# Pooled attention in other tiles (queries 64, 64, 16; keys 128 and 16), and a planner with corrected durations

## The chip, the cores and the metric

The kernel runs on one core of a Trainium2 chip. The metric is the time of one execution on the device in microseconds (us). The engines are TensorE (PE: matmuls, and PEld for its weight loads), VectorE (DVE), ScalarE (ACT), GpSimd (POOL) and the DMA queues, which are issued here by SyncE (SP) and POOL. All inputs and the output are in HBM. PE reads SBUF and writes PSUM; DVE and ACT read and write both.

## The reference

An attention layer over 8 batches, 8 heads, 576 positions and 64 elements a head, and a gated feed-forward network (the code calls it moe) over its 4,608 rows. The weights come as float64.

```python
def _attn_ref(q, k, v):
    factor = 4
    q_d = q.reshape(B, H, Sd, factor, D).mean(axis=3)      # Sd = 144 pooled positions; k_d, v_d likewise
    out_d = sm_attn(q_d, k_d, v_d)                         # softmax attention over the pooled positions
    out_up = np.repeat(out_d, factor, axis=2)
    mask = np.abs(pos[:, None] - pos[None, :]) < factor    # a band of 7 keys
    out_local = softmax(where(mask, scale * q @ k.T, -1e9)) @ v
    return out_up + out_local

def _moe_ref(x, w1, w2, w3, w_out):
    return ((x @ w1) * (x @ w2) @ w3) @ w_out
```

So each row of the network's input is the sum of pooled attention (144 by 144 for each of the 64 batch-heads) and local attention in a band.

## The kernel before, in words

*Network.* `fold` multiplies w3 by w_out once (`accw`, 128 instructions on PE), which leaves one matrix `wphl`. The rows are worked through in 12 chunks of 384 (`moe(c)`). In each, for 8 blocks of the hidden width, PE forms the two gate products (`pab`, L269 to L271, three matmuls per block of the contraction as every operand is split in a high and a low part), ACT copies one (L912), DVE multiplies it with the other (L914), ACT and DVE split the product (L919, L921), and PE multiplies it with `wphl` into `acc`. ACT copies the results (L929) and SP stores them. The split inputs `xh`, `xl` of a chunk are written by two "units" of 192 rows (L861, L862).

*Local attention.* For batches 0 and 1 (`PB`) it is done on PE in groups (`group_unit`, `group_scores`, `group_values`: `se_ps`, `te_ps`, `oe_ps`). These need the queries with the four members of a pool side by side; `turn` in `pooled_sums` makes that order (L559, on ACT). For batches 2 to 7 it is done by `unit` on DVE and ACT: 7 products (L767), reductions (L777, L780), a small softmax, 7 products with v (L826, L834) and their sum, three of the additions being DMAs that POOL issues and that accumulate into `xl` (L842).

*Pooled attention*, the part that is changed. `pooled(b)` brings the sums of q and k over the four members of each pool into `qks` and the sums of v into `vs`: SP issues a first load, POOL three accumulating DMAs (L433, L434; for batches 0 and 1 DVE sums q and k). v lies in `vs` as 72 partitions by 2 halves of the keys. Then `quad` runs twice a batch, for 4 heads each: the scores in three tiles of queries that start at 0, 48 and 80 and are 64 long, two pairs of heads one below the other in 128 partitions, so the tiles overlap (`s_ps`, L482); maxima on DVE (L487), exponentials on ACT with their sums (L496: 6 a quad), the division by the sums on ACT (L508, batches 0 and 1) or POOL (L511); 12 transposes on PE (`t_ps`, L521), because the two halves of 72 keys are transposed apart; and copies into `pt` on ACT (L528). The last step, `values`, multiplies `pt` by v in 32 products over 72 keys (`o_ps`, L449), and ACT copies the result to `oup` (L457, L459).

*Order.* Nothing runs in the order in which it is written. Each piece is a task with an engine, a cost in us, the tasks it needs and the buffers it takes. `Plan.order` simulates the engines with these costs, forward and backward in several rounds, picks the order that its replays find shortest, and the tasks are then issued in that order. Each engine works through its own list in order and waits for semaphores.

Of the kernel before, what the change touches and what calls it, by code (L numbers as in the profile page):

```python
# [32 lines left out]
NT = 3  # L33
THIRDS = [(0, 0), (48, 0), (80, 16)]
# [28 lines left out]
AHEAD = 4  # L63

# [15 lines left out]
class Task:  # L80
    __slots__ = ("eng", "cost", "fn", "deps", "late", "rings", "after")

    def __init__(self, eng, cost, fn, deps, late, rings, after):
        self.eng, self.cost, self.fn, self.deps, self.late, self.rings, self.after = eng, cost, fn, deps, late, rings, after


class Plan:

    def __init__(self):
        self.tasks = []  # L90

    def add(self, eng, cost, fn, deps=(), take=(), uses=(), late=0.0):
# [7 lines left out]
        t = Task(eng, cost, fn, [d for d in deps if d is not None], late, rings, after)  # L100
# [15 lines left out]

    def run(self, prio, slack, back=False, slow=1.0, spare=LATENCY):

# [24 lines left out]
        while best:  # L143
# [32 lines left out]
    def replay(self, order, seed):  # L176
# [14 lines left out]
        return max(end)  # L191

    def order(self):
# [19 lines left out]
        return [self.tasks[i] for i in self.best[3]]  # L213


def dve_us(n, fast=False):
    return (n / 2 if fast else n) / 960 + 0.07


def act_us(n, pointers=0, psum=False):  # L220
    return n / 1200 + (0.045 if psum else 0.09) + 0.093 * pointers
# [18 lines left out]
def tile_attention_moe(ctx: ExitStack, tc: tile.TileContext, q, kw, vw, qk4, v4, w1, w2, w3, wout, edge, out):  # L240
# [15 lines left out]
    nc.scalar.activation(out=junk, in_=junk, func=AF.Exp)  # L256

# [63 lines left out]

    def out_weight(j):
# [7 lines left out]
    def fold():  # L330
# [31 lines left out]

        def part(m, hf):
# [24 lines left out]
    def gate_weights(g):  # L388
# [6 lines left out]
        for wi, wsrc in enumerate((w1, w2)):  # L395
            for k0 in range(0, KT, parts):
                src = wsrc[min(g, 1), k0:k0 + parts, :, at:at + n].rearrange("k p n -> p k n")
                T, ld, tx, wx = words(src, lambda: pools[pool].tile([128, nw], F32, name="wx", bufs=BUFS[pool + "_wx"]), [R[pool + "_wx"]], pool, parts)
                ld.deps += before

                def high(T=T, wi=wi, k0=k0):
                    if gates[wi][g] is None:
                        both = [wpool, pools.get("wlate")][g - 1].tile([128, 2, KT, 2, n], F32R, name=["wo", "wb"][g - 1])
                        for i in range(2):
                            gates[i][g] = both[:, i]
                    T["p"] = gates[wi][g][:, k0:k0 + parts]
                    nc.scalar.copy(out=T["p"][:, :, 0], in_=T["x"].rearrange("p (k n) -> p k n", k=parts))
                th = add("ACT", act_us(nw), high, [tx] + (folded if g == 1 else []), uses=[wx])
                tl = add("DVE", dve_us(nw), lambda T=T: nc.vector.tensor_tensor(out=T["p"][:, :, 1], in0=T["x"].rearrange("p (k n) -> p k n", k=parts), in1=T["p"][:, :, 0].bitcast(F32), op=ALU.subtract), [th], uses=[wx])
                users += [th, tl]  # L410
                g_ready.setdefault((wi, g), []).extend([th, tl])
# [4 lines left out]

    def pooled(b):
# [12 lines left out]
        lv, hv = add("SP", 0.5, first_v, [lq], take=[R["vs"]], late=dma_us(QB * 4096))  # L430
        for f in range(1, FAC):
            if b not in PB:
                lq = add("Pool", 1.04, lambda f=f: nc.gpsimd.dma_start(out=raws[b][0], in_=qk4[b, f], accum_op=ALU.add), [lq], uses=[hq], late=dma_us(128 * 4608, True))  # L433
            lv = add("Pool", 1.04, lambda f=f: nc.gpsimd.dma_start(out=raws[b][1], in_=v4[b, f], accum_op=ALU.add), [lv], uses=[hv], late=dma_us(QB * 4096, True))  # L434
# [8 lines left out]
        def values():  # L443
            for dh in range(2):
                P["o", dh] = ps.tile([128, 2, SD], F32, tag="g", name="o_ps", bufs=BUFS["ps"])
                for par in range(2):
                    for kb in range(2):
                        for Q in range(NQ):
                            nc.tensor.matmul(P["o", dh][32 * Q:32 * Q + 32, par], lhsT=raws[b][1][:, kb, 2 * Q + par, dh * 32:dh * 32 + 32], rhs=P["pt"][:, Q, par, kb], start=kb == 0, stop=kb == 1)  # L449
        tv, *banks = add("PE", 16 * mm_us(2 * SD) + SWITCH, values, pts + [lv], take=[R["ps"], R["ps"]], uses=[hpt, hv])  # L450
        for dh, bank in enumerate(banks):
            def keep(dh=dh):
                if dh == 0:
                    x = work.tile([128, KT * SD], F32, name="oup", bufs=BUFS["oup"])
                    oups[b] = x.rearrange("p (k s) -> p k s", k=KT) if b in PB else x.rearrange("p (s k b) -> p s k b", s=SB, k=KT)
                if b in PB:
                    nc.scalar.copy(out=oups[b][:, 2 * dh:2 * dh + 2], in_=P["o", dh])  # L457
                else:
                    nc.scalar.copy(out=oups[b][:, :, 2 * dh:2 * dh + 2].rearrange("p s a k -> p a s k"), in_=P["o", dh].rearrange("p a (k s) -> p a s k", k=NB))  # L459
# [10 lines left out]

    def quad(b, qd, P, lq, hq, hpt):
        T = {}

        def score():
            for nm in ("mx", "nb", "sm", "rs"):
                T[nm] = small.tile([128, 2, NT], F32, name="g" + nm)
            T["s"] = [ps.tile([128, NT, SD], F32, tag="g", name="s_ps", bufs=BUFS["ps"]) for _ in range(2)]
            for i, (q0, _) in enumerate(THIRDS):
                for w in range(2):
                    for par in range(2):  # L480
                        qk = raws[b][0][par * D:par * D + D, :, 2 * qd + w]
                        nc.tensor.matmul(T["s"][par][w * GQ:w * GQ + GQ, i], lhsT=qk[:, 0, q0:q0 + GQ], rhs=qk[:, 1], start=True, stop=True)  # L482
        sc, *rest = add("PE", 2 * NT * mm_us(2 * SD) + SWITCH, score, [lq], take=[R["ps"], R["ps"], R["gs"]], uses=[hq])
        banks, hg = rest[:2], rest[2]
        mxs = []
        for par in range(2):
            mxs.append(add("DVE", dve_us(NT * SD), lambda par=par: nc.vector.tensor_reduce(out=T["mx"][:, par], in_=T["s"][par], op=ALU.max, axis=AX.X), [sc], uses=[banks[par], hg]))  # L487
        nb = add("DVE", 0.16, lambda: nc.vector.tensor_scalar_mul(T["nb"], T["mx"], -SC), mxs, uses=[hg])
        ex = []
        hp = None  # L490
        slots = [(par, i) for par in range(2) for i in range(NT)]
        for par, i in slots:
            def exp(par=par, i=i):
                if par == i == 0:
                    T["p"] = work.tile([128, 2, NT, SD], F32, name="pexp", bufs=BUFS["p"])
                nc.scalar.activation(out=T["p"][:, par, i], in_=T["s"][par][:, i], func=AF.Exp, bias=T["nb"][:, par, i:i + 1], scale=SC, accum_out=T["sm"][:, par, i:i + 1])  # L496
# [6 lines left out]
        t1 = add("DVE", 0.16, lambda: nc.vector.tensor_scalar(out=T["rs"], in0=T["sm"], scalar1=1e-9, scalar2=float(FAC), op0=ALU.add, op1=ALU.mult), ex, uses=[hg])  # L503
        rs = add("DVE", 0.12, lambda: nc.vector.reciprocal(T["rs"], T["rs"]), [t1], uses=[hg])
        no = []
        if b in PB:
            for par, i in slots:
                no.append(add("ACT", act_us(SD, 1), lambda par=par, i=i: nc.scalar.mul(out=T["p"][:, par, i], in_=T["p"][:, par, i], mul=T["rs"][:, par, i:i + 1]), [rs], uses=[hg, hp]))  # L508
        else:
            for par in range(2):  # L510
                no.append(add("Pool", 1.2, lambda par=par: nc.gpsimd.tensor_tensor(out=T["p"][:, par], in0=T["p"][:, par], in1=T["rs"][:, par].unsqueeze(2).to_broadcast([128, NT, SD]), op=ALU.mult), [rs], uses=[hg, hp]))  # L511
        pts = []

        def flip():
            T["t"] = []
            for i in range(NT):
                T["t"].append(ps.tile([QB, 2, 2, 128], F32, tag="g", name="t_ps", bufs=BUFS["ps"]))
                n = 128 if i == NT - 1 else 128 - GQ + SD // NT
                for par in range(2):
                    for kb in range(2):  # L520
                        nc.tensor.transpose(out=T["t"][i][:, par, kb, :n], in_=T["p"][:n, par, i, kb * QB:kb * QB + QB], identity=ident[:n, :n])  # L521
# [555 lines left out]
```

## Time and profile before

| | |
|---|---|
| median of 3 runs | 782.23 us (782.15 to 783.42) |
| the profiled execution | 783.63 us, its span from first to last instruction 781.9 us |
| mean granted TensorE clock | 0.993 |
| busy: PE, DVE, ACT, POOL | 752.5, 613.0, 540.0, 115.8 us |
| DMA moved | 111.92 MB |

Busy times are sums over the span; an engine that is busy less than the others can still set the time where others wait for it. A group of matmuls overlaps inside PE, so the sum of the durations of its instructions is more than the time it takes; the chain view, which gives the time to the next group, is the one to use for that. In the tables a row "A <- B: 12.2, 4, 8.3" means that A waited 12.2 us in all for B, in 4 places, 8.3 us at the longest.

### The profile page before, as it was taken

How to read it: one execution, taken by the hardware profiler on the slowest of the kernel's cores; microseconds unless marked ns; L12 is line 12 of the kernel's file. 1: busy time of each engine (PE TensorE's matmuls, PEld its weight loads, DVE VectorE, ACT ScalarE, POOL GpSimd, SP SyncE). 2: the span in 40 equal slices, each digit the busy share in tenths (PEclk: the TensorE clock that was granted, in tenths of full speed). 3: DMA queues.
4: the chain of work that ended last, by engine and by line, in shares of the span. 5: the costliest groups of instructions: out<-in, count | busy, mean ns of one | idle time of the engine just before them, and what ended most of it. 6: DMA issues, size and time to landing. Idle time of an engine off the chain costs nothing.

```text
span 781.9 us, 15058 instructions
## 1 busy us (share of the span) xinstructions
PE 752.5 (96%) x5320; PEld 654.8 (84%) x5320; DVE 613.0 (78%) x1049; ACT 540.0 (69%) x2120; POOL 115.8 (15%) x139
## 2 busy tenths in 40 slices
PE   4889999999999999999999999999999999999995
PEld 1445588898999899999999999998999999999994
DVE  4457966749999999989999998998998998963110
ACT  5788898647978688666787686776785787841211
POOL 1000011000221122211121222110221220110000
PEclk9999999999999999999999999999999999999998
DMA  8995779433576727856549739854469544350101
GB/s 291 305 252 182 230 190 218 81 104 103 117 181 177 149 63 202 202 99 171 127 88 224 172 80 216 169 119 135 119 134 224 122 114 120 63 100 1 41 0 41
DMA packets 42548, 111.92 MB, mean 143 GB/s; under 512 B 5080, under 2 KB 11224, under 8 KB 42472
## 3 DMA queue, kind: packets, MB, share of 16 engines
q0 software_dynamic: 12672, 38.94, 28.9%
q1 hardware_dynamic: 29800, 72.01, 28.5%
q8 instruction: 42, 0.69, 0.4%
q14 instruction: 34, 0.28, 0.1%
HBM read 80.26 MB, written 9.44 MB: 115 GB/s over the span
## 4 chain that ended last, share of the span: by engine, by line
PE 73%; issue 7%; DMA 7%; DVE 6%; ACT 5%; POOL 1%; SPq 1%; POOLq 0%; ACTq 0%; DVEq 0%
PE pab L269 14%; PE pab L270 14%; PE pab L271 14%; PE acc L269 7%; PE acc L271 7%; PE acc L270 7%; PE accw L351 3%; DMA raw<-in_w_dram 3%; PE t_ps L521 2%; DMA raw<-in_wout_dram 2%; PE o_ps L449 2%; ACT pexp L496 1%; DVE pr L767 1%; DMA xl<-pv 1%; PE s_ps L482 1%
## 5 line engine op out<-in xcount | busy, mean ns | idle before, releaser
L777 ACT ACTIVATE junk<-pr 128x64 f32<-128x64 f32 x432 | 110.8, 257 | 19.0 <-DVE pr L767 8.4
L767 DVE TENSOR_TENSOR pr<-q_t,kv 128x768 f32<-128x768 f32 x126 | 119.8, 973 | 3.6 <-DMA kv<-in_kw_dram 3.5
L826 ACT ACTIVATE pv<-kv,s_t 128x64 f32<-128x64 f32 x432 | 114.5, 342 | 10.3 <-DVE s_t L803 5.9
L269 PE MATMUL acc<-wphl,gh 128*128 128x512 f32 x288 | 115.5, 401 | 0.0
L271 PE MATMUL acc<-wphl,gl 128*128 128x512 f32 x288 | 113.8, 395 | 0.0
L270 PE MATMUL acc<-wphl,gh 128*128 128x512 f32 x288 | 113.6, 394 | 0.0
L912 ACT COPY a<-pab 128x384 f32<-128x384 f32 x96 | 45.9, 478 | 79.9 <-PE pab L271 66.5
L914 DVE TENSOR_TENSOR a<-pab,a 128x384 f32<-128x384 f32 x96 | 53.2, 554 | 53.5 <-PE pab L271 48.8
L842 POOL DMA_DIRECT2D xl<-pv x54 | 47.2, 875 | 311.4 <-DVE xl L844 249.7
L919 ACT CAST gh<-a 128x384 fp32r<-128x384 f32 x96 | 49.2, 513 | 59.4 <-PE acc L270 52.1
L780 DVE TENSOR_REDUCE s_t<-pr 128x12 f32<-128x768 f32 x90 | 84.1, 944 | 0.1
L777 ACT ACTIVATION_READ_ACCUMULATOR junk<-pr 128x1 f32 x432 | 81.1, 188 | 0.0
L351 PE MATMUL accw<-wo,w 128*128 128x512 f32 x128 | 64.4, 638 | 15.5 <-DVE w L316 12.2
L921 DVE TENSOR_TENSOR gl<-a,gh 128x384 fp32r<-128x384 f32 x96 | 53.9, 562 | 27.9 <-ACT gh L919 27.5
L834 DVE TENSOR_TENSOR pv<-kv,s_t 128x768 f32<-128x768 f32 x72 | 69.8, 979 | 0.1
L269 PE MATMUL pab<-xh,wo 128*128 128x384 f32 x192 | 66.3, 346 | 0.5 <-ACT a L912 0.5
L269 PE MATMUL pab<-xh,w2a 128*128 128x384 f32 x192 | 66.1, 344 | 0.3 <-DVE a L914 0.2
L269 PE MATMUL pab<-xh,w1a 128*128 128x384 f32 x192 | 66.2, 345 | 0.0
L269 PE MATMUL pab<-xh,wb 128*128 128x384 f32 x192 | 65.8, 343 | 0.2
L270 PE MATMUL pab<-xl,w2a 128*128 128x384 f32 x192 | 65.7, 342 | 0.0
L271 PE MATMUL pab<-xh,w2a 128*128 128x384 f32 x192 | 65.5, 341 | 0.0
L271 PEld LDWEIGHTS acc<-wphl,gl 128*128 128x128 f32 x288 | 54.1, 188 | 13.2
(109 smaller groups left out, 1718.6 us busy)
## 6 DMA issues: line engine op xcount, KB each, us to landing
xl<-pv POOLq DMA_DIRECT2D x54, 384.0 KB, 4.3
raw<-in_w_dram SPq DMA_DIRECT2D x32, 512.0 KB
qks<-in_qk_dram POOLq DMA_DIRECT2D x18, 576.0 KB, 7.4
kv<-in_kw_dram SPq DMA_DIRECT2D x18, 576.0 KB
kv<-in_vw_dram SPq DMA_DIRECT2D x18, 576.0 KB
vs<-in_v_dram POOLq DMA_DIRECT2D x24, 288.0 KB, 6.5
q_t<-in_q_dram SPq DMA_DIRECT2D x18, 384.0 KB
out_dram<-o_sb SPq DMA_DIRECT2D x24, 256.0 KB
```

What stands on the lines that cost most here:

```text
L269: nc.tensor.matmul(out_ps, lhsT=lh, rhs=rh, start=first, stop=False)
L270: nc.tensor.matmul(out_ps, lhsT=lh, rhs=rl, start=False, stop=False)
L271: nc.tensor.matmul(out_ps, lhsT=ll, rhs=rh, start=False, stop=last)
L351: nc.tensor.matmul(accs[m], lhsT=T["x"][:, j % 4 * 128:j % 4 * 128 + 128], rhs=wo[0][:, j], start=j == 0, stop=j == NF - 1)
L767: (nc.gpsimd if o in share["qk_pool"] else nc.vector).tensor_tensor(out=T[o], in0=T["q"], in1=T["k"][:, o * D:o * D + nq].rearrange("p (t ...
L777: nc.scalar.activation(out=junk, in_=T[o][:, t], func=AF.Copy, accum_out=T["s"][:, t, o:o + 1])
L780: reds.append(add("DVE", dve_us(nq), lambda o=o: nc.vector.tensor_reduce(out=T["s"][:, :, o], in_=T[o], op=ALU.add, axis=AX.X), [tp], uses ...
L826: nc.scalar.mul(out=T["pv", o][:, tt], in_=T["v"][:, (tt + o) * D:(tt + o + 1) * D], mul=T["s"][:, tt, o:o + 1])
L834: nc.vector.tensor_tensor(out=T["pv", o], in0=T["v"][:, o * D:o * D + nq].rearrange("p (t d) -> p t d", d=D), in1=T["s"][:, :, o].unsqueez ...
L914: tg = add("DVE", dve_us(CT), lambda f=f: nc.vector.tensor_tensor(out=T["a", f], in0=T["p", 1, f], in1=T["a", f], op=ALU.mult), [ta, ends[ ...
L919: nc.scalar.copy(out=T["gh", f], in_=T["a", f])
L921: tl = add("DVE", dve_us(CT), lambda f=f: nc.vector.tensor_tensor(out=T["gl", f], in0=T["a", f], in1=T["gh", f].bitcast(F32), op=ALU.subtr ...
```

## The change

Scores: the queries go in tiles of 64, 64 and, for the last 16, one tile that holds all four pairs of heads in 32 partitions each (it computes the last 32 queries of each and uses 16). Quad 0 has two tiles, quad 1 three. Softmax: the results stand in one fixed buffer `soft` of 320 columns, in which the 144 keys of even heads begin at column 0 and those of odd heads at 176; the last 16 keys of odd heads are also written to columns 160 to 175, and columns 144 to 159 hold zeros. Three transposes of 128 columns a tile (from columns 0, 176 and 128) then give the first 128 keys of both heads and, in the third, the 16 keys left of both. v lies as 128 keys in `vs` and 16 in `vl`, there twice (in partitions 0 and 32). The values are products over 128 keys and over 16. q is turned by DVE. The planner's costs and latencies are changed, and after its search it adds written-out shifts to the priorities of named groups of tasks.

```diff
-NT = 3
-THIRDS = [(0, 0), (48, 0), (80, 16)]
+QM = 64
+QR = SD - 2 * QM
+KR = SD - 128
+KEYS = (0, 160, 176)
...
-LATENCY = 0.18
+LATENCY = 0.09
+DEPTH = dict(PE=0.0)
...
+SHIFTS = [
+    "gates.8.2:2 gates.9.5:-15.5",
+    "down.0.1:-10 down.0.4:21.5 down.0.5:47.5 down.0.7:-65 down.1.1:-12 ..."
...
+]
...
-                can[j] = max(can[j], x + (LATENCY if "PE" not in (e, tasks[j].eng) else 0.0 if e == tasks[j].eng else spare))
+                f = tasks[j].eng
+                can[j] = max(can[j], x + (DEPTH.get(e, 0.04) if e == f else spare if (f if back else e) == "PE" else LATENCY))
...
+    def again(self, prio):
+        now = self.run(prio, 0.1)
+        back = self.run([-x for x in now[2]], 0.05, back=True, slow=1.1)
+        return [-x for x in back[2]]
...
-        return [self.tasks[i] for i in self.best[3]]
+        prio = list(self.best[1])
+        for k, line in enumerate(SHIFTS):
+            if k:
+                prio = self.again(prio)
+            shift = dict((g.replace(".", " "), float(x)) for g, x in (w.split(":") for w in line.split()))
+            prio = [p + shift.get(t.group, 0.0) for p, t in zip(prio, self.tasks)]
+        self.final = self.run(prio, 0.1, slow=1.1)
+        return [self.tasks[i] for i in self.final[3]]

 def dve_us(n, fast=False):
-    return (n / 2 if fast else n) / 960 + 0.07
+    return n / 1920 + 0.155 if fast else n / 960 + 0.1
...
+    soft = wpool.tile([128, 3, KEYS[2] + SD], F32, name="pexp")
+    nc.vector.memset(soft[:, :, SD:KEYS[1]], 0.0)
...
+        def load_v(f, add=False):
+            dma = (lambda **kw: nc.gpsimd.dma_start(accum_op=ALU.add, **kw)) if add else nc.sync.dma_start
+            return [lambda: dma(out=raws[b][1][:QB], in_=v4[b, f, :, 0].rearrange("p h d -> p (h d)")),
+                    lambda: dma(out=raws[b][1][QB:], in_=v4[b, f, :128 - QB, 1].rearrange("p h d -> p (h d)")),
+                    lambda: dma(out=raws[b][2][:KR], in_=v4[b, f, 128 - QB:, 1].rearrange("p h d -> p (h d)"))]
...
-            raws[b][1] = work.tile([QB, 2, H, D], F32, name="vs", bufs=BUFS["vs"])
-            nc.sync.dma_start(out=raws[b][1], in_=v4[b, 0])
+            raws[b][1] = work.tile([128, H * D], F32, name="vs", bufs=BUFS["vs"])
+            raws[b][2] = work.tile([32 + KR, H * D], F32, name="vl", bufs=BUFS["vs"])
+            for ld in load_v(0):
+                ld()
...
+        if b in PB:
+            lv.append(add("DVE", ..., lambda: nc.vector.tensor_copy(out=raws[b][2][32:], in_=raws[b][2][:KR]), ...))
+        else:
+            lv.append(add("ACT", ..., lambda: nc.scalar.copy(out=raws[b][2][32:], in_=raws[b][2][:KR]), ...))
...
+            def product(par, dh, left):
+                if dh == 0 and not left:
+                    P["o", par] = ps.tile([128, 2, SD], F32, tag="g", name="o_ps", bufs=BUFS["ps"])
+                r = slice(32 * par, 32 * par + KR) if left else slice(0, 128)
+                for Q in range(NQ):
+                    h = (2 * Q + par) * D + dh * 32
+                    nc.tensor.matmul(P["o", par][32 * Q:32 * Q + 32, dh], lhsT=raws[b][1 + left][r, h:h + 32], rhs=P["pt"][r, Q, 2 if left else par], start=left == (dh == 1), stop=left == (dh == 0))
+            for dh, left in ((0, False), (0, True), (1, True), (1, False)):
+                for par in range(2):
+                    product(par, dh, left)
...
+        nt = 2 + qd
...
+            for i in range(nt):
+                m, ws, q0 = (32, range(NQ), SD - 32) if i == 2 else (QM, (2 * qd, 2 * qd + 1), QM * i)
+                for w, pair in enumerate(ws):
+                    for par in range(2):
+                        qk = raws[b][0][par * D:par * D + D, :, pair]
+                        nc.tensor.matmul(T["s"][par][w * m:w * m + m, i], lhsT=qk[:, 0, q0:q0 + m], rhs=qk[:, 1], start=True, stop=True)
...
+        no.append(add("DVE", dve_us(nt * KR), lambda: nc.vector.tensor_tensor(out=soft[:, :nt, KEYS[1]:KEYS[2]], in0=T["of"][1][:, :, 128:], in1=wide_(T["rs"][:, :nt, 1], KR), op=ALU.mult), [rs], uses=[hg, hp]))
...
+            for i in range(nt):
+                T["t"].append(ps.tile([128, 3, 128], F32, tag="g", name="t_ps", bufs=BUFS["ps"]))
+                for x, at in enumerate((KEYS[0], KEYS[2], 128)):
+                    nc.tensor.transpose(out=T["t"][i][:, x], in_=T["p"][:, i, at:at + 128], identity=ident)
...
-                    nc.scalar.copy(out=fours[b][qd][0][:, w], in_=x["q"].rearrange("p f s -> p s f"))
+                    nc.vector.tensor_copy(out=fours[b][qd][0][:, w], in_=x["q"].rearrange("p f s -> p s f"))
```

The other costs are changed in the same way as `dve_us` (for instance 1.04 us to 0.9 for a DMA that POOL issues, and for the values from 16 times the price of 288 columns plus 0.19 us to 1.48 + 0.22 + 0.19 us).

More of the change, by code (lines that the diff above doesn't have):

```diff
@@ L90, in __init__, with named, run @@
         self.tasks = []
+        self.group = ""
+    def named(self, fn):
+        def run(*a):
+            old, self.group = self.group, " ".join([fn.__name__] + [str(x) for x in a if isinstance(x, int)])
+            r = fn(*a)
+            self.group = old
+            return r
+        return run
     def add(self, eng, cost, fn, deps=(), take=(), uses=(), late=0.0):
@@ L99, in add @@
             after += last[:1]
-        t = Task(eng, cost, fn, [d for d in deps if d is not None], late, rings, after)
+        t = Task(eng, cost, fn, [d for d in deps if d is not None], late, rings, after, self.group)
         for h in list(got) + list(uses):
@@ L115, in link, with run @@
                 self.then[at[d]].append(i)
-    def run(self, prio, slack, back=False, slow=1.0, spare=LATENCY):
+    def run(self, prio, slack, back=False, slow=1.0, spare=0.22):
         tasks = self.tasks
@@ L394, in gate_weights @@
         parts = 512 // n
-        for wi, wsrc in enumerate((w1, w2)):
-            for k0 in range(0, KT, parts):
[L397 to L411, printed above, removed]
@@ new lines, in gate_block, with high @@
+        @plan.named
+        def gate_block(g, wi, k0):
+            src = (w1, w2)[wi][min(g, 1), k0:k0 + parts, :, at:at + n].rearrange("k p n -> p k n")
+            T, ld, tx, wx = words(src, lambda: pools[pool].tile([128, nw], F32, name="wx", bufs=BUFS[pool + "_wx"]), [R[pool + "_wx"]], pool, parts)
+            ld.deps += before
+            def high():
+                if gates[wi][g] is None:
+                    both = [wpool, pools.get("wlate")][g - 1].tile([128, 2, KT, 2, n], F32R, name=["wo", "wb"][g - 1])
+                    for i in range(2):
+                        gates[i][g] = both[:, i]
+                T["p"] = gates[wi][g][:, k0:k0 + parts]
+                nc.scalar.copy(out=T["p"][:, :, 0], in_=T["x"].rearrange("p (k n) -> p k n", k=parts))
+            th = add("ACT", act_us(nw), high, [tx] + (folded if g == 1 else []), uses=[wx])
+            tl = add("DVE", dve_us(nw), lambda: nc.vector.tensor_tensor(out=T["p"][:, :, 1], in0=T["x"].rearrange("p (k n) -> p k n", k=parts), in1=T["p"][:, :, 0].bitcast(F32), op=ALU.subtract), [th], uses=[wx])
+            users.extend([th, tl])
+            g_ready.setdefault((wi, g), []).extend([th, tl])
@@ L414, in tile_attention_moe @@
+        for wi in range(2):
+            for k0 in range(0, KT, parts):
+                gate_block(g, wi, k0)
     oups, oup_ready, oup_held, raws = {}, {}, {}, {}
     pep = []
+    @plan.named
     def pooled(b):
@@ L443, in values, with keep @@
         def values():
-            for dh in range(2):
-                P["o", dh] = ps.tile([128, 2, SD], F32, tag="g", name="o_ps", bufs=BUFS["ps"])
-                for par in range(2):
[L447 to L453, printed above, removed]
+            def product(par, dh, left):
[6 more added lines that the diff above has]
+            for dh, left in ((0, False), (0, True), (1, True), (1, False)):
+                for par in range(2):
+                    product(par, dh, left)
+        tv, *banks = add("PE", 1.48 + 0.22 + SWITCH, values, pts + lv, take=[R["ps"], R["ps"]], uses=[hpt, hv])
+        for par, bank in enumerate(banks):
+            def keep(par=par):
+                if par == 0:
                     x = work.tile([128, KT * SD], F32, name="oup", bufs=BUFS["oup"])
@@ L787, in mask @@
                 nc.vector.tensor_tensor(out=T["s"][:, ts, os_], in0=T["s"][:, ts, os_], in1=edge_sb[:, e], op=ALU.add)
-            last = [add("DVE", 0.19, mask, last, uses=[hs])]
+            last = [add("DVE", 0.24, mask, last, uses=[hs])]
         def top():
@@ L827, in unit @@
                     if t0 == 0:
-                        tm, h = add("ACT", TOKENS * act_us(D, 1), mult, [soft, lv], take=[ring], uses=[hv, hs])
+                        tm, h = add("ACT", TOKENS * act_us(D, 1), mult, [norm, lv], take=[ring], uses=[hv, hs])
                     else:
@@ L836, in mult @@
                         in1=T["s"][:, :, o].unsqueeze(2).to_broadcast([128, UT, D]), op=ALU.mult)
-                tm, h = add("DVE", dve_us(nq), mult, [soft, lv], take=[ring], uses=[hv, hs])
+                tm, h = add("DVE", dve_us(nq), mult, [norm, lv], take=[ring], uses=[hv, hs])
             if i == 0:
@@ L924, in moe @@
         for f, d, hg in lag:
+            plan.group = f"down {c} {f}"
             down(f, d, hg)
```

129 lines of the change are left out of this document (79 added, 50 removed).

## The prediction

> **What bounds the kernel now.** I read the page's busy time and slices first, then busy time by stage, then what TensorE (PE) waited for, then the two ends of the span.
>
> ```profile
> span 781.9 us, 15058 instructions
> ...
> PE 752.5 (96%) x5320; PEld 654.8 (84%) x5320; DVE 613.0 (78%) x1049; ACT 540.0 (69%) x2120; POOL 115.8 (15%) x139
> ...
> PE   4889999999999999999999999999999999999995
> ```
>
> Busy time by stage; the columns are the stretch and its length, then PE, weight loads, VectorE (DVE), ScalarE (ACT), GpSimd (POOL), granted clock, DMA share, GB/s:
>
> ```profile
> 27.00:46.00 19.00, 15.25 (x64) 6.75 (x64) 10.76 (x27) 16.27 (x51) 1.82 (x2) 1.00 1.00 312
> ...
> 120.00:200.00 80.00, 78.94 (x972) 69.94 (x972) 57.67 (x130) 55.63 (x223) 6.82 (x7) 1.00 0.46 121
> 200.00:400.00 200.00, 200.00 (x1255) 185.11 (x1254) 187.02 (x288) 150.17 (x660) 38.00 (x42) 1.00 0.63 145
> 400.00:600.00 200.00, 199.52 (x1316) 182.20 (x1315) 184.78 (x285) 150.74 (x653) 44.30 (x46) 1.00 0.69 159
> ```
>
> From 120 us on PE has no holes: 200.00 of 200, then 199.52 of 200. A microsecond taken off PE there can come off the span. DVE stands right behind it with 187.02 and 184.78 of 200, so it has little room. PE's holes lie in the first 46 us, where DMA is at 1.00 of its time and the weights arrive one block after another:
>
> ```profile
> PE accw L351 <- DVE w L316: 12.2, 4, 8.3
> PE accw L351 <- DVE wo L316: 3.3, 2, 2.1
> ```
>
> That is 15.5 us of waiting for weights, 8.3 of it before the first matmul; 7.2 us are left that an order could move. The chain that ended last shows ACT in one such wait: exponentials, the conversion of a weight block, then the matmul.
>
> ```profile
> 42.24 1.46 ACT pexp L496 x8
> ...
> 45.51 0.70 DVE w L316
> 46.26 1.98 PE accw L351 x4
> ```
>
> At the other end, the last matmul, the last copy of a result, the last unit of local attention that DVE finishes (L862), and PE's matmuls on `pab` before 700 us and from there to 713 us:
>
> ```profile
> 772.16 0.40 PE L271 MATMUL acc<-wphl,gl 128*128 128x512 f32 x1
> 775.90 0.58 ACT L929 COPY o_sb<-acc 128x512 f32<-128x512 f32 x1 [3.41 <-DMA out_dram<-o_sb]
> ```
> ```profile
> L862 DVE TENSOR_TENSOR xl<-xt,xh x18: 945/952/960, 257.5 to 711.9; 128x768 fp32r<-128x768 f32 x18
> ```
> ```profile
> 0.00:700.00 700.00, 388.57 (x2052) 1.00 0.63 157
> 700.00:713.00 13.00, 9.34 (x48) 1.00 0.17 30
> ```
>
> PE ends at 772.6 us; 9.3 us of copies and stores follow, which no edit touches. DVE ends its last unit at 711.9 + 0.95 = 712.9 us. By then PE has done 2,100 of its 2,304 gate matmuls, so 192 of the last chunk and 12 of the one before are left. The last chunk can't start before that unit. 772.6 - 712.9 = 59.7 us remain, and the chunk itself takes about 50 (worked out below). So the end has two conditions: PE's sum of work, and DVE's last unit plus 50 us, with some 9.6 us between them. A saving on PE beyond those 9.6 us would need DVE to be done earlier.
>
> **The change, part by part: PE.** The chain view gives the time from the first instruction of a group to the next group; the timeline shows the neighbours of the value products:
>
> ```profile
> 163.59 0.66 PE te_ps L626 x6
> 165.65 1.49 PE oe_ps L697 x96
> ...
> 200.65 1.21 PE t_ps L521 x12
> 204.30 0.90 PE s_ps L482 x24
> 246.78 2.10 PE o_ps L449 x64
> ```
> ```profile
> 246.27 0.34 PE L270 MATMUL pab<-xl,w2a 128*128 128x384 f32 x1
> 246.44 0.34 PE L271 MATMUL pab<-xh,w2a 128*128 128x384 f32 x1
> 246.71 2.17 PE L449 MATMUL o_ps<-pt,vs 72*32 72x144 f32 x64
> 248.81 0.44 PE L269 MATMUL pab<-xh,wo 128*128 128x384 f32 x1
> 249.09 0.34 PE L270 MATMUL pab<-xl,wo 128*128 128x384 f32 x1
> ```
>
> Gate matmuls start 0.17 us apart (246.27 to 246.44); before and after the value products the step is 0.27 and 0.28 us (246.44 to 246.71, 248.81 to 249.09). So entering and leaving a group of small tiles costs 0.20 us together, and one change of tile shape about 0.10. (With 0.175 us for a gate matmul and, in the ratio 512/384, 0.233 for a down matmul, a chunk is 192 x 0.175 + 72 x 0.233 = 50.4 us, the 50 above.)
>
> Each product or score matmul is two instructions in the trace. `o_ps` (64 instructions, 144 columns) took 2.10 us and `oe_ps` (96 of 64 columns) 1.49. With a price per column p and a fixed part: 9216 p + fixed = 2.10, 6144 p + fixed = 1.49, so 144 columns cost 0.0286 us and the fixed part is 0.27. `s_ps` agrees: 24 x 0.0286 + 0.2 = 0.90.
>
> Transposes. Before, two quads of 12, 2 x 1.21 = 2.42 us a batch. `te_ps` gives 0.66 / 6 = 0.11 us for a transpose 128 wide. After, 6 and 9 of them: 15 x 0.11 = 1.65, so -0.77 us. Not shown before is a transpose whose stationary side has 128 columns instead of 72. Bounds: 0.11 if the load stays hidden, and 0.175, the step of the gate matmuls, which load 128 columns each; then 15 x 0.175 = 2.63, +0.2. I take 0.11: the six rows nearest are transposes too.
>
> Scores. Before 2 x 0.90. After, quad 0 has 8 matmuls, 16 x 0.0286 + 0.25 = 0.71. Quad 1 has those and 8 on tiles of 64x32, with one change of shape: 0.46 + 16 y + 0.25 + 0.10. If eight tiles of half size run at once where four ran, y is 0.0143, otherwise 0.0286. `oe_ps` starts instructions 1.49 / 96 = 0.0155 us apart, so PE can issue at about that pace; I take the first. 0.71 + 1.04 = 1.75, -0.05 us; the other end is +0.18, and with shape changes free it is -0.15.
>
> Values. Before 2.10. After, 16 products over 128 keys and 16 over the 16 keys left, on tiles of 32x32 in two row groups: 32 x 0.0286 + 32 y + 0.25 + two changes of 0.10 = 1.83, -0.27 us; with the slow y 2.29, +0.19; with free changes -0.47.
>
> Per batch -0.77 - 0.05 - 0.27 = -1.09 us, times 8 = -8.7; the ends are 8 x -1.39 = -11.1 and 8 x 0.57 = +4.6. Batch 0's scores and first transposes run before 46 us among the waits for weights, so 0.44 of it buys nothing: **-8.3 us**.
>
> The Trainium skill, "TensorEngine Tiling (Array Packing)", section "Key Properties", states that changing the tiling mode drains the engine. It speaks against the mixed shapes; the 0.10 us a change is what this trace shows of it, and no run here yet shows a change between two small shapes back to back. If it costs as much as the whole fixed part, 0.27 instead of 0.10, three changes a batch add 0.5 us, and the PE sum would be -4.6 instead of -8.7.
>
> **ACT and DVE.**
>
> ```profile
> L496 ACT ACTIVATE pexp<-s_ps,gnb 128x144 f32<-128x144 f32 x96 | 35.4, 386 | 2.4 <-DVE gnb L488 2.0
> L496 ACT ACTIVATION_READ_ACCUMULATOR pexp<-s_ps,gnb 128x1 f32 x96 | 20.2, 211 | 0.0
> L528 ACT COPY pt<-t_ps 72x384 f32<-72x384 f32 x48 | 20.0, 474 | 0.0
> L559 ACT COPY qn<-q 128x576 f32<-128x576 f32 x8 | 9.3, 1175 | 2.8 <-DMA q<-in_qk_dram 2.8
> ```
> ```profile
> L767 DVE TENSOR_TENSOR pr<-q_t,kv 128x768 f32<-128x768 f32 x126 | 119.8, 973 | 3.6 <-DMA kv<-in_kw_dram 3.5
> L487 DVE TENSOR_REDUCE gmx<-s_ps 128x3 f32<-128x432 f32 x32 | 18.0, 599 | 1.9 <-PE s_ps L482 1.8
> L787 DVE TENSOR_TENSOR s_t<-s_t,edge_sb 128x9 f32<-128x9 f32 x12 | 2.6, 218 | 0.0
> ```
>
> ACT loses 16 exponentials with their reads (16 x 0.6 = 9.6 us), 8 copies of `t_ps` and half of 8 more (5.7), and the turn of q (9.3); it gains six copies of the 16 rows of v (about 0.5 each, as a 384-wide copy is 0.474). DVE gains the 8 turns (576 of 768 elements of a 0.973 us operation, 0.7 each, 5.8 us, all in the first 130 us where it has room: 10.76 of 19 us), a small multiply per quad (0.2 each by the 9-element row), and two copies of v. It loses a third of the two maxima of quad 0, 2 x 0.2. In the full stretch that is 2 x 0.2 - 0.4 = 0 a batch: DVE is neither helped nor hurt there. ACT is no bound; what it gains on the path is in the first 46 us, where two exponentials fewer per quad 0, the turns and the copies stand ahead of weight conversions. Of the 7.2 us of waits that are left there I take **-1.0**; the ends are 0 and -7.2 from what the rows show, and a worse order can lose as much.
>
> **POOL, SP and the queues.**
>
> ```profile
> L842 POOL DMA_DIRECT2D xl<-pv x54 | 47.2, 875 | 311.4 <-DVE xl L844 249.7 <-DVE mx L792 16.8 <-DVE s_t L787 16.7
> L511 POOL TENSOR_TENSOR pexp<-pexp,grs 128x432 f32<-128x432 f32 x24 | 29.6, 1261 | 93.5 <-ACT pv L826 51.7 <-DVE grs L504 29.6 <-ACT junk L777 11.6
> L434 POOL DMA_DIRECT2D vs<-in_v_dram x24 | 22.9, 956 | 139.0 <-DMA vs<-in_v_dram 138.0 <-PE pab L271 0.9
> ```
> ```profile
> POOL vs L434 <- DMA vs<-in_v_dram: 138.0, 14, 52.3
> ```
> ```profile
> DVE xl L844 <- DMA xl<-pv: 6.7, 4, 3.3
> ```
>
> The sums over v become 9 DMAs a batch instead of 3: 6 x 0.956 = 5.7 us more on POOL's queue, less 1.1 for the narrower multiplies (four of 1.26, down by a fifth). POOL is at 44.3 of 200, so it can carry 4.6 us in 80. But it works in order, and behind a v sum that waits for the one before (138.0 us in all) stand the sums into `xl` that DVE needs; DVE waits 6.7 us for those now. I cost this at nothing because the three pieces of one step are independent and wait together, and because POOL waits on DVE for most of its time (249.7 us); if that cover goes, DVE's last unit slips. SP issues three first loads instead of one, with nothing close behind them. The new order itself (corrected durations, shifts of groups) I cost at zero on PE after 120 us, where there is no hole to close.
>
> **Sum.** The profiled execution took 783.6 us, 1.7 outside its span; 783.6 - 8.3 - 1.0 = 774.3. It stands 1.4 above the median of 782.2, so the forecast is **773.0** (772.9). PE's last matmul would end at 763.3, and 50 us earlier, at 713, DVE's last unit must be done: that is today's 712.9. From here on a slip of DVE costs its full length.
>
> **Rivals.** (1) *The start gives more.* DVE has only 57.67 of 80 us in 120:200, as units wait for the end of the exact-attention groups. Lighter ACT and PE work there can start the stream of units earlier, and the waits for weights shrink. With the PE end of -11.1 and half the 7.2 us: 783.6 - 11.1 - 3.6 - 1.4 = 767.5; further down only with DVE done before 709. (2) *Narrow tiles do not pay:* slow y, so -0.77 + 0.18 + 0.19 = -0.40 a batch, -3.2 - 1.0: 778. (3) *POOL's queue holds DVE back, and the end is slower than before.* Place: the six later batches, 4.6 us of POOL each, 28 in all, ahead of `xl` sums. If DVE's end slips by a third of it, 9.3 us, it eats the 9.3 saved and nothing is gained; by half, 14 us, the time is 773 + 14 = 787. For it speaks that DVE is at 94%; against it, that POOL's idle time is mostly its waiting for DVE. The skill's "DMA: Bandwidth & Descriptors", section "Anatomy of one DMA — SWDGE (gpsimd) path", puts about 2 us of fixed time on each such DMA whatever its size; were the pieces served one after another, 6 more a batch are an estimated 12 us of added latency. No run here shows pieces of 32 KB on that queue.
>
> **Chances.** Forecast 0.50 (769 to 777); rival 1 0.20 (762 to 769); rival 2 0.12 (777 to 780.5); DVE slips by just what was saved, no change, 0.06; rival 3 0.12. Anything within 0.2% (780.7 to 783.8) a measurement can't tell from no change. So faster 0.82, same 0.06, slower 0.12. The range 763 to 782 leaves out rival 3 and the ends of the others, under 0.2.
>
> **What would show it.** Right: `t_ps` groups of 6 and 9 at 0.66 and 0.99 us, `o_ps` at 1.8 and `s_ps` at 0.7 and 1.0; PE busy down by 8 to 9 us; PE still at 200 of 200 in mid-span; DVE's last unit at or before 713. Wrong: `o_ps` above 2.1 (rival 2); DVE waiting more than 6.7 us for `xl` sums, or PE waiting for `xh` or `xl` (rival 3); more than 15.5 us of PE waits for weights.

## The result, and the profile after

Nine runs of the changed kernel had a median of 773.1 us (769.2 to 779.0), against 782.5 us (781.0 to 783.6) for the kernel before, run beside it: a ratio of 0.988, 95% interval 0.985 to 0.991. The forecast was 773.0 us. The profiled execution took 773.75 us with a span of 771.9. The runs scatter more than those of the kernel before beside them (10 us against 3); beside the experiments below that kernel's own runs spread over 7 to 11 us, so the scatter is not put down to the change.

The page of the changed kernel, busy time and PE's slices:

```profile
span 771.9 us, 14990 instructions
...
PE 739.4 (96%) x5248; PEld 640.1 (83%) x5248; DVE 618.3 (80%) x1076; ACT 525.5 (68%) x2074; POOL 153.2 (20%) x187
...
PE   3899989999999999999999999999999999999994
```

PE is busy 13.1 us less, in a span 10.0 us shorter. The stages and PE's waits (columns as before):

```profile
27.00:46.00 19.00, 16.39 (x81) 7.72 (x78) 10.29 (x29) 16.78 (x49) 5.98 (x7) 1.00 0.96 276
...
120.00:200.00 80.00, 78.56 (x969) 69.82 (x968) 57.72 (x129) 54.87 (x214) 12.42 (x14) 1.00 0.42 108
200.00:400.00 200.00, 199.65 (x1274) 183.06 (x1273) 190.19 (x297) 153.09 (x666) 49.07 (x56) 1.00 0.67 151
400.00:600.00 200.00, 196.98 (x1286) 178.99 (x1285) 186.30 (x291) 147.90 (x639) 55.27 (x62) 0.99 0.70 160
```
```profile
PE accw L408 <- DVE w L370: 13.3, 4, 8.4
PE pab L323 <- ACT a L1010: 3.9, 5, 1.8
PE se_ps L749 <- issue: 1.4, 1, 1.4
PE accw L408 <- DVE wo L370: 1.2, 2, 0.7
PE acc L325 <- DVE gl L1019: 0.9, 1, 0.9
```

Two things are new. PE has holes in the middle, 3.0 us between 400 and 600, where it waits for ACT and DVE between the gates. And the waits for weights are 14.5 us, where 15.5 stood. The groups of the pooled attention, from the chain view:

```profile
216.41 0.66 PE t_ps L609 x6
227.87 1.06 PE s_ps L566 x32
243.13 0.98 PE t_ps L609 x9
246.20 1.90 PE o_ps L527 x64
...
278.20 0.65 PE s_ps L566 x16
...
390.77 1.17 PE s_ps L566 x32
```

Transposes take 0.66 + 0.98 us, scores 0.65 + 1.06 (1.17 in two places), values 1.90: 5.25 us a batch where 6.32 stood, so -1.07, and -8.6 for eight. The end of the span, PE's last matmul, the last copy, and DVE's last unit:

```profile
761.69 0.39 PE L325 MATMUL acc<-wphl,gl 128*128 128x512 f32 x1
765.37 0.59 ACT L1028 COPY o_sb<-acc 128x512 f32<-128x512 f32 x1 [3.35 <-DMA out_dram<-o_sb]
```
```profile
L958 DVE TENSOR_TENSOR xl<-xt,xh x18: 948/954/960, 257.6 to 702.4; 128x768 fp32r<-128x768 f32 x18
```

PE ends at 762.1 us, 10.5 earlier. DVE's last unit ends at 703.4 us, 9.5 earlier, although DVE has 5 us more to do: it follows PE. (In e1 below, where only PE gets more to do, both come later by 2.4 us.)

**Where the 10.5 us come from.** A chunk's work on PE is 0.175 us for each `pab` matmul and 0.233 for each `acc` one, 604.5 us in all. What PE has done of it by 200 us divides the span in a start and a steady part. First the kernel before, then the changed one; in each the row of `pab`, then that of `acc`:

```profile
0.00:200.00 200.00, 62.12 (x312) 0.99 0.67 192
0.00:200.00 200.00, 22.76 (x85) 0.99 0.67 192
```
```profile
0.00:200.00 200.00, 65.49 (x333) 1.00 0.66 193
0.00:200.00 200.00, 25.20 (x96) 1.00 0.66 193
```

That is 312 x 0.175 + 85 x 0.233 = 74.4 us of chunk work before, and 80.6 after: the start is worth 6.2 us. From 200 us to PE's end the kernel before spent 572.6 us on the 530.1 that were left, 42.5 on other things; the changed kernel 562.1 on 523.9, 38.2: the steady part gives 4.3. Six batches at 1.07 us would be 6.4; the new holes (3.4 us between 200 and 600 where 0.5 stood) and the slow clock behind one of them (1.7 us, last section) are more than enough for the rest.

The start did not gain by fewer holes: up to 200 us PE stands idle for 19.6 us before and 19.4 after. Of its 6.2 us, about 2.1 are the lighter groups of batches 0 and 1 (2 x 1.07). Another 1.7 (0.39 + 0.50 + 0.50 + 0.31) are a slow stretch of the kernel before, which the trace of the changed one does not have. It stands behind two waits of PE for ACT, 1.23 and 0.53 us:

```profile
99.99 0.39 PE L521 MATMUL t_ps<-ident,pexp 112*72 112x112 f32 x2 [1.23 <-ACT pexp L508]
```
```profile
102.00:103.00 1.00, 1.00 (x6) 1.00 (x5) 0.99 (x2) 1.00 (x3) 0.00 (x0) 0.61 1.02 326
103.00:104.00 1.00, 1.00 (x5) 1.00 (x5) 0.30 (x1) 1.00 (x3) 0.65 (x1) 0.50 1.07 381
...
105.00:106.00 1.00, 1.00 (x12) 0.57 (x14) 0.19 (x1) 0.74 (x2) 0.00 (x0) 0.69 1.13 336
```

These are one trace of each kernel, so it is not shown that every execution has this difference. The other 2.4 us are not taken apart.

### The profile page after: what moved, and what is told of

Same layout as the page of the kernel before. It is cut to its first block, busy times and chain, and to the rows that moved or that the text cites. A ratio compares the mean times of both kernels' runs of the same rounds, so it can differ in the third digit from the quotient of the medians.

```text
span 771.9 us, 14990 instructions
## 1 busy us (share of the span) xinstructions
PE 739.4 (96%) x5248; PEld 640.1 (83%) x5248; DVE 618.3 (80%) x1076; ACT 525.5 (68%) x2074; POOL 153.2 (20%) x187
## 4 chain that ended last, share of the span: by engine, by line
PE 75%; DMA 9%; DVE 7%; ACT 5%; issue 3%; POOL 0%; SPq 0%; DVEq 0%; ACTq 0%; POOLq 0%
PE pab L323 15%; PE pab L325 15%; PE pab L324 15%; PE acc L323 7%; PE acc L325 7%; PE acc L324 7%; DMA raw<-in_w_dram 4%; DMA kv<-in_kw_dram 2%; DMA out_dram<-o_sb 2%; PE accw L408 2%; DVE pr L863 2%; PE o_ps L527 1%; PE s_ps L566 1%; PE t_ps L609 1%; DMA xl<-pv 1%
## 5 line engine op out<-in xcount | busy, mean ns | idle before, releaser
L922 ACT ACTIVATE pv<-kv,s_t 128x64 f32<-128x64 f32 x432 | 111.0, 338 | 12.1 <-DVE s_t L899 6.5
L408 PE MATMUL accw<-wo,w 128*128 128x512 f32 x128 | 62.1, 621 | 14.4 <-DVE w L370 13.3
L323 PE MATMUL pab<-xh,wb 128*128 128x384 f32 x192 | 66.1, 344 | 2.1 <-ACT a L1010 2.1
L323 PE MATMUL pab<-xh,w2a 128*128 128x384 f32 x192 | 65.2, 340 | 0.5 <-DVE a L1012 0.5
L325 PE MATMUL pab<-xh,wb 128*128 128x384 f32 x192 | 65.2, 339 | 0.0
L324 PE MATMUL pab<-xl,wb 128*128 128x384 f32 x192 | 65.2, 339 | 0.0
L324 PE MATMUL pab<-xl,w1a 128*128 128x384 f32 x192 | 64.9, 338 | 0.3
```

Source lines behind the costliest of these rows:

```text
L323: nc.tensor.matmul(out_ps, lhsT=lh, rhs=rh, start=first, stop=False)
L324: nc.tensor.matmul(out_ps, lhsT=lh, rhs=rl, start=False, stop=False)
L325: nc.tensor.matmul(out_ps, lhsT=ll, rhs=rh, start=False, stop=last)
L408: nc.tensor.matmul(accs[m], lhsT=T["x"][:, j % 4 * 128:j % 4 * 128 + 128], rhs=wo[0][:, j], start=j == 0, stop=j == NF - 1)
L922: nc.scalar.mul(out=T["pv", o][:, tt], in_=T["v"][:, (tt + o) * D:(tt + o + 1) * D], mul=T["s"][:, tt, o:o + 1])
```

## The experiments

In each, the order of every engine's list stays that of the changed kernel unless it is said that it was planned anew. The kernel before ran beside each of them. The ratios of the changed kernel and of most experiments are good to 0.003, so a distance from the changed kernel, in us below, is good to about 3 us, and to about 5 in e4 and e8.

**e1: PE's work put back.** Does a microsecond on PE count?

```diff
-                    nc.tensor.transpose(out=T["t"][i][:, x], ...)
+                    for _ in range(2 if (qd == 0 or i == 0) else 1):
+                        nc.tensor.transpose(out=T["t"][i][:, x], ...)
```

> The changed kernel with the same order on every engine, but each quad transposes its first tiles twice, so 12 transposes a quad as before instead of 6 and 9: 9 more a batch at 0.11 us, 0.99 us of PE a batch, 7.9 us in all (about 7.3 on the path, as part of batch 0's falls among the waits for weights). Theory (PE's sum of work sets the time): about 7 us slower than the changed kernel, ratio to the kernel before 0.997. Rival (the gain came from the new order and its costs, PE has room): less than 2 us slower, ratio 0.988 to 0.990.

Ratio 0.995 (0.992 to 0.997): 0.0069 more than the changed kernel, 5.4 us. A group of 12 took 1.31 us, so the dose was 7.8 us, about as planned.

```profile
555.94 1.31 PE t_ps L610 x12
```
```profile
400.00:600.00 200.00, 199.04 (x1316) 181.19 (x1315) 187.13 (x292) 149.29 (x646) 56.70 (x63) 1.00 0.71 161
```

The rival (no more than 2 us) is out. Whether the 7.3 us on the path counted in full can't be told from 5.4; some of it may have gone into holes, as PE is at 199.04 of 200 here, where the changed kernel has 196.98.

**e2: DVE's work raised.** Each maximum of the pooled scores is taken twice.

```diff
-  nc.vector.tensor_reduce(out=T["mx"][:, :nt, par], ...)
+  [nc.vector.tensor_reduce(out=T["mx"][:, :nt, par], ...) for _ in range(2)]
```

> The changed kernel with the same order, but DVE takes each maximum of the pooled scores twice: 2 x 0.449 + 2 x 0.604 = 2.1 us of DVE a batch, 16.8 us in all, 12.6 of it in the six later batches. As the prediction has it (from the changed kernel on a slip of DVE costs its full length): about 12 us slower than the changed kernel, ratio 1.003. Rival (DVE is paced by PE and has some 8 us of room at its last unit): 4 us slower or less, ratio under 0.993.

Ratio 0.997 (0.994 to 1.000), 7.2 us slower than the changed kernel: between the two. That is 0.57 us for each of the 12.6 added in the later batches, or 0.43 for each of all 16.8; with the error of 3 us, a third to four fifths of the 12.6.

```profile
PE pab L323 <- ACT a L1010: 5.3, 9, 1.0
```
```profile
200.00:400.00 200.00, 197.38 (x1256) 179.50 (x1254) 190.75 (x301) 148.02 (x650) 46.93 (x54) 1.00 0.64 148
400.00:600.00 200.00, 195.41 (x1278) 176.23 (x1279) 189.55 (x300) 148.87 (x645) 55.82 (x61) 1.00 0.70 161
```

DVE's added work reaches PE as more waits for the gates' products: 9 of them and 5.3 us, where the changed kernel has 5 and 3.9, though none is longer than 1.0 us. Between 200 and 600 us PE is busy 3.8 us less than in the changed kernel. So added work on either engine costs time here: the changed kernel has used up most of the room that DVE had.

**e3: POOL's work raised** by a scratch write after each sum over v.

```diff
-  lv = [add("Pool", 0.9, ld, [t], ...
+  lv = [add("Pool", 0.9, lambda ld=ld: (ld(), nc.gpsimd.memset(spin, 0.0)), [t], ...
```

> The changed kernel with the same order, but POOL writes a scratch tile of 128x432 after each of the 72 sums over v, 0.46 us each, 33 us in all, 25 of it in the six later batches: about the POOL time that the 48 added DMAs cost, once more. Theory (POOL's queue is covered, it mostly waits for DVE): under 1.5 us slower than the changed kernel, ratio 0.988 to 0.990. Rival 3 of the prediction (POOL's queue holds DVE back): a third to a half of 25 us, 8 to 12 us slower, ratio about 1.0.

Ratio 0.990 (0.987 to 0.992), 1.4 us above the changed kernel, within the scatter. POOL's busy time rose from 153 to 184 us and the time hardly moved: the cover that the prediction named holds in this order, and rival 3 has no ground here.

**e4: a third buffer for results,** against the 3.35 us that the last copy waits.

```diff
-  pools["mp"].tile([128, DM], F32, name="o_sb", bufs=BUFS["o"])
+  pools["mp"].tile([128, DM], F32, name="o_sb", bufs=3)
```

> The changed kernel with the same order and three buffers for results instead of two. In the trace the last copy of a result waits 3.35 us for a store to free its buffer, after PE's last matmul. Theory (that wait lies on the end of the chain): 3 to 4 us faster than the changed kernel, ratio 0.983 to 0.984. Rival (the last store lands as late behind the others whatever the copy does): no change, ratio 0.988.

Ratio 0.988 (0.982 to 0.994): no change to be told, though with this scatter the time alone doesn't rule out 3 us. The trace does. The wait is gone, as the three copies now run on end:

```profile
759.69 1.94 ACT L1028 COPY o_sb<-acc 128x512 f32<-128x512 f32 x3 [2.17 <-PE acc L325]
```
```profile
766.00:768.00 2.00, 0.00 (x0) 0.00 (x0) 0.00 (x0) 0.00 (x0) 0.00 (x0) 0.50 0.44 128
768.00:770.00 2.00, 0.00 (x0) 0.00 (x0) 0.00 (x0) 0.00 (x0) 0.00 (x0) 0.50 0.15 59
```

The copies end at 761.6 us, but the stores still move data at 768 to 770 us, and the span ends 9.9 us after PE's last matmul, where it was 9.8 in the changed kernel. The theory fell; what is left to set the end is the stores' own pace (128 GB/s and less).

**e5: the new tiles with the planner's old latencies and formulas** (its other new costs stay); planned anew.

```diff
-LATENCY = 0.09          (and the other latencies, dve_us, act_us)
+LATENCY = 0.18          (as in the kernel before)
-        ... shifts of groups ...
-        return [self.tasks[i] for i in self.final[3]]
+        return [self.tasks[i] for i in self.best[3]]
```

> The new tiles, transposes, v rows and the turn on DVE, but the planner's latencies and its DVE and ACT formulas as before and no shifts of groups; the order is planned anew from these. Theory (the gain is PE's lighter pooled attention, the planner adds nothing after 120 us): most of the gain, ratio to the kernel before 0.988 to 0.991. Rival (the corrected durations and the shifts made the gain): ratio 0.996 or more.

Ratio 1.003 (1.000 to 1.006): the whole gain is gone, 11.8 us above the changed kernel. This is the worst miss of all that was expected. The waits, the stretch after the longest, chunk work done by 200 us (`pab`, then `acc`), and the last stretch:

```profile
PE o_ps L517 <- DMA vs<-in_v_dram: 4.7, 1, 4.7
PE pab L313 <- ACT xh L799: 2.5, 1, 2.5
PE pab L314 <- DVE xl L800: 2.2, 1, 2.2
```
```profile
124.00:128.00 4.00, 0.32 (x2) 0.00 (x0) 1.84 (x5) 1.76 (x8) 0.00 (x0) 1.00 0.90 238
128.00:132.00 4.00, 2.99 (x64) 1.80 (x64) 0.00 (x0) 0.12 (x1) 0.00 (x0) 0.66 0.87 192
132.00:136.00 4.00, 4.00 (x39) 2.89 (x32) 1.81 (x4) 1.75 (x4) 0.87 (x1) 0.50 0.64 131
```
```profile
0.00:200.00 200.00, 57.12 (x279) 0.96 0.64 185
0.00:200.00 200.00, 20.14 (x72) 0.96 0.64 185
```
```profile
740.00:800.00 60.00, 36.44 (x186) 33.11 (x184) 6.14 (x11) 7.23 (x14) 0.00 (x0) 0.94 0.07 18
```

By 200 us 279 x 0.175 + 72 x 0.233 = 65.6 us of chunk work are done, 8.8 less than before the change and 15.0 less than in the changed kernel. From there to PE's end at 776.4 us it spends 37.5 us on other things, 5.0 less than the kernel before. So the tiles bring their gain in the steady part under either planner, and the start decides the rest: in this order PE stands 9.4 us in three waits between 96 and 130 us, and the granted clock falls after them (0.66 and 0.50 above). Up to 200 us PE stands idle for 27.7 us, 8.4 more than in the changed kernel. From 46 to 200 us the share of the clock that was not granted, summed over PE's busy time, comes to 7.1 us, and to nothing in the changed kernel. Together that is about the 15.0.

**e6: the planner's new durations with the old tiles;** planned anew, no shifts.

```diff
-LATENCY = 0.18
+LATENCY = 0.09          (and DEPTH, spare, dve_us, act_us, 0.9 for POOL's DMAs)
```

> The kernel before with the new planner latencies, DVE and ACT formulas and POOL costs, no shifts (they are written for the new tasks). Theory: PE has no hole after 120 us that an order could close, so ratio 0.998 to 1.003. Rival (the new durations find a better order): ratio 0.995 or less.

Ratio 1.005 (1.002 to 1.009): slower, if anything, by more than the theory's 1.003. The durations are no gain by themselves with the old tiles.

**e7: the changed kernel without the shifts;** planned anew.

```diff
-            shift = dict(...)      (and the passes with it)
+        return [self.tasks[i] for i in self.best[3]]
```

> The changed kernel without the written-out shifts; the order is the one that its search finds with the corrected durations. Theory: like the changed kernel, ratio 0.987 to 0.990. Rival (the shifts carry part of the gain, by fewer holes on PE): ratio 0.992 or more, with PE waiting several us more than the changed kernel's 21.

Ratio 0.991 (0.988 to 0.994), 2.7 us above the changed kernel, and the two intervals overlap. Against e5, the order that the search finds with the corrected latencies and formulas is worth 9 us with the new tiles; the shifts at most a few. In the trace of e7 PE has done 76.3 us of chunk work by 200 us and spends 37.7 on other things after that; in that of e6, with the old tiles, 74.9 and 44.8. So over five orders the steady part takes 42.5 and 44.8 us with the old tiles, 37.5, 37.7 and 38.2 with the new (36 to 41 in the other traces without added work on PE or DVE): that part of the gain is the tiles'. The start goes with the order. Each set of durations was tried with one order only, and other durations can send the search to another one. So it is shown that these orders differ by 9 us, but not that it is the better durations, rather than the draw, that make it so.

**e8: q turned on ACT again.**

```diff
-  nc.vector.tensor_copy(out=fours[b][qd][0][:, w], ...)
+  nc.scalar.copy(out=fours[b][qd][0][:, w], ...)
```

> The changed kernel with the same order, but the 8 turns of q are done by ACT again, 1.175 us each, at the places in the order where DVE does them. Theory (ACT stands ahead of weight conversions in the first 46 us, worth about 1.0 us): 0 to 2 us slower than the changed kernel, ratio 0.988 to 0.991. Rival (the turns' place decides the start): 4 us or more, ratio 0.993 and up.

Ratio 0.989 (0.984 to 0.994), 0.8 us above the changed kernel: of the size expected, but with an error of 5 us neither nothing nor the rival's 4 us is ruled out.

**e9 and e10: v's sums of batch 1 left out,** in the order of e5 and, as a control, in that of the changed kernel.

```diff
-  lv = [add("Pool", 0.9, ld, [t], ...
+  lv = [add("Pool", 0.9, ld if b != 1 else (lambda: None), [t], ...
```

> The kernel of e5 (new tiles, old latencies and formulas, no shifts) with the same order, without the 9 accumulating DMAs of v of batch 1: that batch's v is only the first of four members, the rest is computed as before. In e5 PE waited 4.7 us for the last of these at 124 us, and the granted clock fell to 0.66 and 0.50 in the 8 us after it. Theory (e5 lost its gain by such waits before 200 us and the slow clock behind them): 5 to 9 us faster than e5, ratio to the kernel before 0.991 to 0.997. Rival (another wait takes that place, or the loss lies elsewhere): within 2 us of e5, ratio 1.000 to 1.005.

> The control of e9: the changed kernel with the same order, without the same 9 DMAs. There PE does not wait for v. Theory: within 1 us of the changed kernel, ratio 0.986 to 0.990. Rival (these DMAs slow the weights' and keys' loads): 3 us faster or more, ratio 0.984 or less.

e9: ratio 0.996 (0.993 to 0.998), 5.6 us faster than e5. e10: 0.987 (0.984 to 0.990), 0.9 us faster than the changed kernel, not to be told from nothing. In e9 the group of values of batch 1 starts at 122.4 us without a wait, and PE is full there at full clock:

```profile
122.40 1.91 PE o_ps L517 x64
```
```profile
120.00:140.00 20.00, 20.00 (x330) 16.15 (x328) 14.38 (x35) 17.02 (x61) 6.29 (x8) 1.00 0.82 189
```

So one late chain of sums over v cost e5 about half of its 11.8 us (5.6, good to 3). The rest (the two waits near 100 us for `xh` and `xl`, and what follows them) was not tested by a run, nor which of the old durations leads the search to such an order.

**e11: the multiply of the last 16 keys on POOL** for the later batches.

```diff
-  nc.vector.tensor_tensor(out=soft[:, :nt, KEYS[1]:KEYS[2]], ...)
+  (nc.vector if b in PB else nc.gpsimd).tensor_tensor(out=soft[:, :nt, KEYS[1]:KEYS[2]], ...)
```

> The changed kernel with the same order, but for the six later batches the multiply of the last 16 keys (128x32 and 128x48) is done by POOL instead of DVE: 12 operations, 6 x 0.313 + 6 x 0.465 = 4.7 us off DVE, as much onto POOL. If DVE is worth in this stretch what e2 showed (7.2 us for 12.6, 0.57 each), 2.7 us faster than the changed kernel, ratio 0.984 to 0.985. Rival (DVE's slack is used up only when it gets slower): no change, ratio 0.987 to 0.989. If POOL's queue delays the transposes: slower.

Ratio 0.987 (0.984 to 0.990), 0.4 us faster than the changed kernel: no change to be told, and the 2.7 us are not ruled out either. The trace gives the rival some ground: PE stands idle for 3.0 us between 200 and 600 us here, and for 3.4 in the changed kernel, so hardly any of its holes closed.

**e12: one more change of tile shape.**

```diff
-  for dh, left in ((0, False), (0, True), (1, True), (1, False)):
+  for dh, left in ((0, False), (0, True), (1, False), (1, True)):
```

> The changed kernel with the same order, but the four parts of the value products go 128 keys, 16 keys, 128 keys, 16 keys instead of 128, 16, 16, 128, so the tile shape changes three times instead of two inside the group. The changed kernel's group takes 1.90 us. At 0.10 us a change, as the prediction has it: 2.00. If a change costs the whole fixed part, 0.27: 2.17.

The group took 2.06 us instead of 1.90, so 0.16 us a change, between the two. Its parts in the timeline:

```profile
56.84 0.70 PE L527 MATMUL o_ps<-pt,vs 128*32 128x144 f32 x16
57.47 0.47 PE L527 MATMUL o_ps<-pt,vl 16*32 16x144 f32 x16
57.87 0.70 PE L527 MATMUL o_ps<-pt,vs 128*32 128x144 f32 x16
58.50 0.47 PE L527 MATMUL o_ps<-pt,vl 16*32 16x144 f32 x16
58.90 1.12 PE L408 MATMUL accw<-wo,w 128*128 128x512 f32 x2
```

From start to start 16 instructions of the small tile take 0.40 us here, and 32 of them took 0.65 in the changed kernel (0.63 for each part of 16 on 128 keys and 1.90 for the group): 16 more for 0.25, 0.0156 us each. The smaller tiles run at about half the price of the larger, as the prediction took it; rival 2 is out.

## Why the prediction was right, and where only its sum was

The time came out at 773.1 for 773.0, but not all of its steps did.

- *PE's work.* Transposes -0.77 a batch, measured -0.78; scores -0.05, measured -0.09; values -0.27, measured -0.20; sum -8.7, measured -8.6. The change of shape was taken as 0.10 us and is 0.16 (e12), the small tile's instruction as 0.0143 and is 0.0156. That PE's work sets the time is borne out by e1, at 5.4 us for 7.8. The Trainium skill, "TensorEngine Tiling (Array Packing)", section "Key Properties", has the engine drain at each change; the 0.16 us agrees with that, and its price leaves the narrow tiles worth having.
- *POOL at nothing:* right in this order (e3). The pieces of v of 144, 112 and 32 KB landed in a median of 4.9, 5.7 and 4.4 us, where one of 288 KB took 6.5, and POOL waited 124.5 us for the piece before, instead of 138.0. In the order of e5 the same sums came late, and PE waited 4.7 us for them.
- *DVE at 0 a batch:* a little too low. The small multiplies took 0.31 and 0.47 us, not 0.2 each, and the maxima gave back 0.30, not 0.4: +0.5 us a batch.
- *The turn and ACT at the start, -1.0:* not settled; e8 shows 0.8 for the turn, with an error of 5.
- *"The new order itself I cost at zero on PE after 120 us":* this is the step that failed, and with it the -1.0 as the only term for the start. After 120 us an order couldn't close holes, as there were none, but it could open them there, and before 200 us it could open or avoid them: in the order that the old durations gave, the new tiles gain nothing (e5). In the changed kernel the start gives 6.2 us where the prediction's terms (batches 0 and 1, and 1.0) come to about 2.7. About half of that difference is the slow stretch at 102 us. The prediction had no term for it: it put PE's holes in the first 46 us, though PE misses another 3.4 us between 46 and 120.
- *"From here on a slip of DVE costs its full length":* too strong. DVE's last unit moved from 712.9 to 703.4 us with PE, and added DVE work cost about 0.57 of its length (e2). The condition at 713 us was no limit, as DVE is itself paced by the gates that PE delivers.
- *No holes in mid-span:* wrong by 3.4 us of 400, and one of them has a tail of slow clock, below. PE's busy time fell by 13.1 us, not by the 8 to 9 named as a sign, and only 8.6 of it are the groups counted here. PE also waited 0.6 us for `xh`, which was named as a sign of rival 3.

The start came out 3.5 us better than the terms of the prediction, and the steady part, with 4.3 where six batches at 1.09 would give 6.5, 2.2 worse. PE's last matmul moved by 10.5 us where 9.3 were forecast. So the mechanism, PE's lighter work, was right, but that the sum came out to a tenth of a microsecond is luck: two errors of opposite sign, and a scatter of several us from run to run.

## What to carry to other kernels

Where one engine is full over most of the span, count its instructions stage by stage from the groups in the chain view: that gave each term here within 0.1 us a batch. But a planned order is part of the kernel: in the order that the old durations gave, the same tiles lost all of the gain in the first 200 us, by waits and by the slow clock behind them, so look at where PE first runs dry, not only at where it is full. Before adding to the second-busiest engine, raise its work once in a fixed order; here 12.6 us added to DVE in the later batches cost about 7, so little of its room was left.

## What the runs showed of the hardware

A wait of PE can cost more than its length. In the changed kernel one of 1.84 us is followed by a granted clock of a half for about 3.4 us, in which gate matmuls start 0.32 us apart instead of 0.175: about 1.7 us more. The matmul after the wait, and the stretch in steps of one microsecond:

```profile
427.29 0.44 PE L323 MATMUL pab<-xh,wb 128*128 128x384 f32 x1 [1.84 <-ACT a L1010]
```
```profile
426.00:427.00 1.00, 0.00 (x0) 0.00 (x0) 1.00 (x3) 0.24 (x1) 0.00 (x0) 1.00 0.85 157
...
428.00:429.00 1.00, 1.00 (x6) 1.00 (x5) 1.00 (x3) 0.88 (x2) 1.00 (x2) 0.77 0.49 73
429.00:430.00 1.00, 1.00 (x5) 1.00 (x5) 1.00 (x2) 0.17 (x2) 0.55 (x1) 0.50 0.65 62
...
431.00:432.00 1.00, 1.00 (x5) 1.00 (x4) 1.00 (x2) 0.97 (x6) 0.07 (x1) 0.53 0.72 117
432.00:433.00 1.00, 1.00 (x8) 1.00 (x7) 0.96 (x2) 0.94 (x6) 0.59 (x1) 1.00 0.24 35
```

Not every wait is followed by this. In the same trace one of 1.4 us (`se_ps`, at 139 us) is not: the granted clock is 1.00 from there to 400 us. Nor is one of 2.85 us for weights, after which 16 matmuls take 7.13 us, 0.45 each, as in the groups after it (12 in 5.42 us):

```profile
17.48 7.13 PE L408 MATMUL accw<-wo,w 128*128 128x512 f32 x16 [2.85 <-DVE w L370]
```

The Trainium skill, "TensorE: Matmul & The Clock Gate", section "Part 1: The HAM clock gate", has the clock fall to a half after an idle window of about 3.4 us, and rise again after a busy one as long. The length of the slow stretch agrees (in e5 two of them, from 102 and from 129 us, are twice as long); the wait that set it off was 1.84 us, little more than half of that, while the longer one of 2.85 us set off none, and here the measurement decides. What decides which waits are followed by the slow clock is not shown by these runs.
